# Where the first chunk's ELU takes its second step: VectorE's clamp against ScalarE's Relu, in an attention and feed-forward kernel

## The chip, the cores and the metric

One core of one Trainium2 chip. The metric is the device time of one execution in microseconds, as the median of several runs. TensorE is PE in the profile, VectorE is DVE, ScalarE is ACT, GpSimd is POOL; PEld is PE's loading of weights, SP issues DMAs.

## The reference, cut to what matters

```
# attention over q, k, v (4 x 8 heads x 768 x 64), window 16, plus 24 block summaries
a = exp(scores_all - max); a = a / (sum(a) + 1e-09); x = a @ v_all        # -> x (3072, 512)
# feed-forward
h = x @ w_in                                                               # (3072, 2048)
g = where(h > 0, h, exp(minimum(h, 0)) - 1)                                # ELU
out = g @ w_out                                                            # (3072, 512)
```

## The kernel before, in words

The 3072 rows of x are worked in six chunks of 512. For each chunk the 2048 hidden columns are taken in 16 tiles f of 128. One tile is 12 matmuls of 512 columns into the PSUM tile `h` (layer 1), the ELU from `h` to the SBUF tile `e`, the split of `e` into a rounded part `gh` and a rest `gl`, and 12 matmuls of layer 2 that add to four output banks. Every product is made of three, from high and low parts of both operands.

The first chunk is different from the other five. In its time the 32 weight tiles (j = 0 to 31; tile f uses j = 2f-1 in layer 1 and j = 2f+2 in layer 2) are still being loaded and converted: POOL makes the low bits (word `X.j`, line 136), ACT scales the exponent into a PSUM bank (`M.j`, line 141), DVE joins both (`S.j`, lines 145 and 148), ACT (three times POOL) rounds the high part (`H.j`, line 154), POOL subtracts for the low part (`L.j`, line 157). In between, the attention of the coming chunks runs in groups g of two units with halves h: `gsc` scores on PE (531), `glow` mask and minimum on DVE (168), `ge` exponentials and their sums on ACT (176), `gz` adds 1e-9 and takes the reciprocal of the sums on DVE (181, 182), `gn` scales the rows on POOL (185), `gtr` transposes on PE (194), `gpc` copies them from PSUM (550), `gval` the values on PE (567), `gxh` and `gxl` the split of the result on ACT and DVE (574, 581). Scores and transposes use the same two PSUM banks (`a0`, `a1`) as the exponent step `M.j`, so each must be read out before the other writes.

In this chunk the order of every engine's queue is the order of the words of the string `FIRST` (lines 40 to 72), written out by hand; line 730 runs them. The words of a tile f are, with the functions that they call:
- `L1h.f`, `L1l.f` (`layer1_part`, 614): 8 and 4 matmuls with the weight's high and low part.
- `E.f` (`take_exp`, `exp_of`, 619): ACT, e = exp(h).
- `ts.f` (`below`, 623): DVE, e = min(e, 1) - 1.
- `stt.f` (`above`, 626): DVE, e = max(h, 0) + e.
- `G.f` (`split_high`, 631): ACT, gh = e rounded. `gl.f` (`split_rest`, 636): POOL, gl = e - gh.
- `L2a.f`, `L2b.f`, `L2c.f` (`layer2_part`, 646): 4 matmuls each, with gh and the weight's high part, with gl and the high part, with gh and the low part. The words stand in the order a, c, b in the first tiles and mostly a, b, c later.

Tiles `e`, `gh`, `gl` and `cv` have two buffers each. From tile 16 on (chunks 1 to 5, the loop from line 748) the same functions `exp_of`, `below`, `above`, `split_high` and `split_rest` are called; there only PE and SP keep the program's order, and a planner orders the other engines. `exps` (line 172) and `exp` of the first units (line 349) allocate the tile `z` for the sums of exponentials.

Of the kernel before, what the change touches and what calls it, by code (L numbers as in the profile page):

```python
# [17 lines left out]
F32 = mybir.dt.float32  # L18
# [14 lines left out]
UW = 4  # L33
# [12 lines left out]
    tr.2.0 q.1 mv.0.1.1 z.3 ptc.2.0.1 X.0 w.5 tr.2.1 mv.1.2.1 X.1 tr.1.0 ptc.2.1.1 val.0 norm.3.0 ptc.1.0.0 M.0  # L46
    M.1 S.0 norm.3.1 val.1 mv.0.3.1 xh.0 w.6 X.2 S.1 tr.3.0 xh.1 X.3 tr.3.1 ptc.3.0.1 sk.1 X.4 val.2 ptc.3.1.1
    xl.0 H.0.1 w.7 xl.1 val.3 xh.2 H.1.1 xl.2 L.0 w.8 first.0 xh.3 M.2 xl.3 L.1 first.1 M.3 sk.2 S.2 first.2 X.5
    w.9 first.3 S.3 H.2.1 M.4 L1h.1 E.0 L.2 w.10 ts.0 H.3 stt.0 L.3 L1l.1 sk.3 S.4 G.0 E.1 gl.0 L2a.0 w.11 M.5
    L2c.0 M.6 S.5 X.6 H.4 w.12 L2b.0 X.7 ts.1 H.5 L.4 L1h.2 sv.0 M.7 stt.1 L.5 w.13 G.1 S.6 L1l.2 gl.1 S.7 L2a.1  # L50
    H.6 w.14 L2c.1 L.6 H.7 sv.1 L2b.1 E.2 ks.3 L.7 K.2 vm.0 vm.1 gsc.0 ts.2 X.8 stt.2 L1h.3 X.9 glow.0.0 G.2
    X.10 glow.0.1 M.8 gl.2 ge.0.0 L1l.3 S.8 q.2 L2a.2 w.15 X.11 E.3 gz.0.0 X.12 L2c.2 H.8 ts.3 w.16 M.9 L.8
    L2b.2 stt.3 M.10 S.9 L1h.4 G.3 sv.2 gn.0.0 ge.0.1 S.10 gl.3 L1l.4 gz.0.1 L2a.3 E.4 gn.0.1 M.11 ts.4 L2c.3
    H.9 stt.4 H.10 L2b.3 L.9 vs.1 G.4 gtr.0.0 L.10 L1h.5 S.11 gl.4 ks.2 H.11 L1l.5 gpc.0.0.1 ks.0 L.11 M.12
    gtr.0.1 ks.1 L2a.4 gpc.0.1.1 X.13 M.13 S.12 L2b.4 X.14 E.5 L2c.4 pm.2 S.13 H.12 pm.3 gval.0 X.15 X.16 ts.5
    H.13 gsc.1 w.17 w.18 sv.3 L.12 stt.5 w.19 G.5 L1h.6 glow.1.0 L.13 gxh.0 glow.1.1 M.14 w.20 gl.5 gxl.0 L1l.6
    M.15 ge.1.0 S.14 w.21 L2a.5 L2b.5 S.15 E.6 w.22 H.14 L2c.5 X.17 ts.6 H.15 L.14 L1h.7 w.23 M.16 gz.1.0 stt.6
    M.17 L.15 S.16 w.24 G.6 L1l.7 ge.1.1 gl.6 L2a.6 S.17 K.3 E.7 X.18 L2b.6 H.16 gz.1.1 gn.1.0 ts.7 L2c.6 L.16
    stt.7 gtr.1.0 vs.2 L1h.8 G.7 q.3 gn.1.1 H.17 vs.0 w.25 gpc.1.0.1 gl.7 vs.3 M.18 L1l.8 S.18 w.26 gtr.1.1 E.8
    X.19 L2a.7 gpc.1.1.1 L.17 ts.8 M.19 w.27 L2b.7 stt.8 X.20 L2c.7 S.19 G.8 X.21 w.28 gval.1 gl.8 w.29 gsc.2  # L60
    gxh.1 X.22 H.18 gxl.1 H.19 L1h.9 L.18 glow.2.0 w.30 M.20 L.19 w.31 ge.2.0 L1l.9 S.20 X.23 L2a.8 glow.2.1 E.9
    X.24 L2b.8 H.20 ts.9 ge.2.1 L.20 L2c.8 stt.9 gz.2.0 mmul G.9 L1h.10 gz.2.1 mact mm gl.9 M.21 M.22 S.21
    L1l.10 gn.2.0 L2a.9 gn.2.1 S.22 M.23 E.10 L2b.9 X.25 H.21 ts.10 X.26 L2c.9 H.22 stt.10 L.21 gtr.2.0 G.10
    L1h.11 gpc.2.0.1 L.22 S.23 M.24 L1l.11 gl.10 S.24 H.23 gtr.2.1 L.23 L2a.10 gpc.2.1.0 H.24 L2b.10 M.25 L.24
    E.11 S.25 L2c.10 X.27 gval.2 K.4 q.4 ts.11 X.28 H.25 stt.11 L.25 gsc.3 G.11 gxh.2 L1h.12 gl.11 glow.3.1
    glow.3.0 ge.3.1 gxl.2 X.29 L1l.12 X.30 M.26 L2a.11 gz.3.1 E.12 gn.3.1 S.26 L2b.11 ge.3.0 L2c.11 ts.12 H.26
    stt.12 L1h.13 M.27 L.26 G.12 S.27 M.28 gl.12 L1l.13 gz.3.0 M.29 L2a.12 S.28 gn.3.0 E.13 H.27 L2b.12 X.31
    ts.13 H.28 L2c.12 L.27 stt.13 gtr.3.0 L.28 L1h.14 S.29 gpc.3.0.1 M.30 G.13 S.30 L1l.14 H.29 gl.13 gtr.3.1
    L2a.13 L.29 gpc.3.1.1 M.31 L2b.13 H.30 S.31 L2c.13 E.14 L.30 gval.3 ts.14 stt.14 gsc.4 gxh.3 H.31 gxl.3 G.14
    L1h.15 L.31 glow.4.0 ge.4.0 gl.14 L1l.15 L2a.14 E.15 ts.15 L2b.14 stt.15 L2c.14 glow.4.1 G.15 gl.15 ge.4.1  # L70
    gz.4.1 gz.4.0 gn.4.1 gn.4.0
"""
# [3 lines left out]
def attn_elu_ffn(ctx: ExitStack, tc: tile.TileContext, qT, kT, vT, v, w_in, w_out, out):  # L76
    nc = tc.nc
    B, NP, _, S = qT.shape
# [13 lines left out]
    scale = 1.0 / math.sqrt(D)  # L92
# [3 lines left out]
    att = ctx.enter_context(tc.tile_pool(name="att", bufs=2))  # L96
# [74 lines left out]

    def exps(sm, mx, z=None):
        if z is None:
            z = att.tile([P, UW, 1], F32, tag="z", name="z", bufs=4)
        for t in range(UW):
            nc.scalar.activation(out=sm[:, t, :], in_=sm[:, t, :], func=AF.Exp, bias=mx[:, t, :], scale=-1.0,  # L176
                                 accum_out=z[:, t, :])
        return z
# [27 lines left out]
    def put_maxima(b, p):  # L206
        nc.gpsimd.tensor_copy(out=kw[p][:, :, KB:KC], in_=ks_all[b][:, p:p + 1, :].broadcast_to([P, UW, NS]))
# [9 lines left out]
    def first_units():  # L217
# [5 lines left out]
        ks = ks_all[0]  # L223
# [15 lines left out]
        mxs, zs, banks_of, o_of = {}, {}, {}, {}  # L239
# [349 lines left out]
    hs = {}  # L589
# [101 lines left out]
    with tc.manual_schedule(engines=set(engines.values())):  # L691
        do = first_units()
        convs, sources, es = {}, {}, {}
        copies = (nc.vector.tensor_copy, nc.scalar.copy)

        def conversion(j):
            if j not in convs:
                convs[j] = Conversion(j)
            return convs[j]

        def load_sum(p, src):
            sources[src is vT, p] = load_summary(1, p, src, spares[src is vT][p])

        def take_exp(n):
            es[n] = exp_of(hs[n])

        do |= {
            "w": lambda j: load(order[j]), "q": load_queries, "sk": lambda p: load_sum(p, kT),
            "sv": lambda p: load_sum(p, vT),
            "K": group_windows,  # L710
            "pm": lambda g: [put_maxima(1, units[2 * g][1] + i) for i in range(2)],
            "ks": lambda p: summary(1, p, kT, sources.pop((False, p))),
            "vs": lambda p: summary(1, p, vT, sources.pop((True, p))),
            "mmul": lambda: mean_products(1, "a1"), "mact": lambda: mean_copy(1),
            "mm": lambda: [put_means(1, p, vw[p]) for p in range(NP)],
            "X": lambda j: conversion(j).low_bits(), "M": lambda j: conversion(j).exponent(),
            "S": lambda j: conversion(j).join(), "H": lambda j, pool=0: conversion(j).high(nc.gpsimd.tensor_copy if pool else nc.scalar.copy),
            "L": lambda j: conversion(j).rest(),
            "L1h": lambda n: layer1_part(n, 0), "L1l": lambda n: layer1_part(n, 1),
            "L2a": lambda n: layer2_part(n, 0), "L2b": lambda n: layer2_part(n, 1), "L2c": lambda n: layer2_part(n, 2),  # L720
            "E": take_exp, "ts": lambda n: below(es[n]), "stt": lambda n: above(es[n], hs[n]),
            "G": lambda n: split_high(0, n, es[n]), "gl": lambda n: split_rest(0, n, es[n]),
            "gsc": group_scores, "glow": group_low, "ge": group_exps,
            "gz": lambda g, h: reciprocals(z_of[g, h]), "gn": lambda g, h: scale_rows(sm_of[g, h], z_of.pop((g, h))),
            "gtr": group_transposes, "gpc": lambda g, h, i: group_copy(g, h, copies[i]),
            "gval": group_values, "gxh": group_high, "gxl": group_rest,
        }
# [17 lines left out]
    with tc.manual_schedule(engines={engines["PE"], engines["SP"]}):  # L745
        pending = None
        last = NCH * NF - 1
        for n in range(NF, NCH * NF):
            c, f = divmod(n, NF)
            g, step = divmod(n, 4)  # L750
            h_ps = layer1(c, f)
            e = exp_of(h_ps)
# [14 lines left out]
            if n in summaries:  # L767
                b, p, src = summaries[n]
# [62 lines left out]
```

## Time and profile before

| | us |
|---|---|
| median of 3 runs | 626.95 (626.69 to 627.38) |
| the profiled execution | 626.43 |
| its span in the profile | 624.7 |
| PE busy | 616.7 (99% of the span) |
| DVE busy | 268.4 (43%) |
| ACT busy | 272.7 (44%) |
| POOL busy | 249.5 (40%) |

PE's busy time is modelled and covers waits shorter than its pipeline; where PE really stood is read from the starts of its matmuls. The shares of the other engines are means over a first fifth in which they are nearly full and a remainder in which they are about a third full.

### The profile page before, as it was taken

The numbers are of one execution on the slowest core, as the hardware profiler recorded it, in microseconds if no ns is written. First come the engines' busy times: TensorE is split into PE (matmuls) and PEld (weight loads), VectorE is DVE, ScalarE is ACT, GpSimd is POOL, SyncE is SP. The second block draws the span as 40 slices with busy tenths as digits, with TensorE's granted clock in tenths as the row PEclk, the third lists the DMA queues.
The fourth block names the chain that finished last, engine by engine and source line by source line (L and its number), as shares of the span: only waits on it lengthen the run. The fifth ranks groups of instructions, "written<-read, shape, count | busy, mean of one in ns | idle before, by whom it ended". The sixth has DMA issues, their size and how long they took to land.

```text
span 624.7 us, 11284 instructions
## 1 busy us (share of the span) xinstructions
PE 616.7 (99%) x4251; PEld 503.3 (81%) x4251; DVE 268.4 (43%) x853; ACT 272.7 (44%) x745; POOL 249.5 (40%) x266
## 2 busy tenths in 40 slices
PE   9999999999999999999999999999999999999997
PEld 6678778888888888888888888888888888888885
DVE  7789988743153432331543433314323232211222
ACT  5858676754243343442434434425334333222222
POOL 4999899742232332323323323233233231222221
PEclk9999999999999999999999999999999999999999
DMA  8998962142004405220053132402211000100001
GB/s 319 337 383 255 292 236 74 38 133 54 11 27 142 117 28 173 68 64 1 27 155 119 42 101 60 117 0 73 82 45 40 2 1 0 68 0 1 1 0 67
DMA packets 63549, 58.62 MB, mean 94 GB/s; under 512 B 22648, under 2 KB 54904, under 8 KB 63496
## 3 DMA queue, kind: packets, MB, share of 16 engines
q1 hardware_dynamic: 60184, 52.02, 27.3%
q10 hardware_dynamic: 3312, 5.90, 2.6%
q8 instruction: 33, 0.54, 0.4%
q14 instruction: 20, 0.16, 0.1%
HBM read 50.82 MB, written 6.29 MB: 91 GB/s over the span
## 4 chain that ended last, share of the span: by engine, by line
PE 86%; DVE 3%; issue 1%; ACT 0%; DVEq 0%; ACTq 0%
PE h L603 36%; PE o L656 35%; PE h L614 3%; PE o_ps L567 3%; PE o L646 3%; PE s L531 3%; PE t_ps L194 3%; DVE sh L145 1%; DVE e L623 1%; DVE cv L148 0%; DVE vst L495 0%; DVE e L626 0%; DVE z L181 0%; DVE sm L168 0%; DVE xl L581 0%
## 5 line engine op out<-in xcount | busy, mean ns | idle before, releaser
L636 POOL TENSOR_TENSOR gl<-e,gh 128x512 fp32r<-128x512 f32 x96 | 123.7, 1289 | 278.5 <-ACT gh L631 209.2
L603 PE MATMUL h<-xh,w 128*128 128x512 f32 x640 | 214.1, 395 | 0.0
L656 PE MATMUL o<-w,gh 128*128 128x512 f32 x648 | 164.7, 392 | 0.0
L623 DVE TENSOR_SCALAR e<-e 128x512 f32<-128x512 f32 x96 | 46.6, 485 | 253.6 <-ACT e L619 252.0
L603 PEld LDWEIGHTS h<-xh,w 128*128 128x128 f32 x640 | 120.1, 188 | 27.0 <-issue 2.4
L656 PEld LDWEIGHTS o<-w,gh 128*128 128x128 f32 x648 | 120.5, 188 | 24.3
L619 ACT ACTIVATE e<-h 128x512 f32<-128x512 f32 x96 | 56.9, 592 | 166.7 <-PE h L603 159.7
L603 PE MATMUL h<-xl,w 128*128 128x512 f32 x320 | 124.5, 389 | 0.0
L631 ACT CAST gh<-e 128x512 fp32r<-128x512 f32 x96 | 59.6, 621 | 97.2 <-DVE e L626 97.1
L656 PE MATMUL o<-w,gl 128*128 128x512 f32 x324 | 89.6, 389 | 0.0
L656 PEld LDWEIGHTS o<-w,gl 128*128 128x128 f32 x324 | 60.8, 188 | 12.7
L185 POOL TENSOR_TENSOR sm<-sm,z 128x480 f32<-128x480 f32 x40 | 42.8, 1073 | 67.9 <-DVE z L182 33.3
L603 PEld LDWEIGHTS h<-xl,w 128*128 128x128 f32 x320 | 60.2, 188 | 11.4
L626 DVE SCALAR_TENSOR_TENSOR e<-h,e 128x512 f32<-128x512 f32 x96 | 66.4, 691 | 3.3
L176 ACT ACTIVATE sm<-sm,mx 128x120 f32<-128x120 f32 x160 | 61.0, 383 | 15.3 <-DVE mx L168 15.3
L157 POOL TENSOR_TENSOR w<-cv,w 128x512 fp32r<-128x512 f32 x32 | 41.8, 1322 | 5.4 <-ACT w L154 4.6
L614 PE MATMUL h<-xh,w 128*128 128x512 f32 x120 | 40.5, 399 | 0.0
L581 DVE TENSOR_TENSOR xl<-o_ps,xh 128x256 fp32r<-128x256 f32 x40 | 15.1, 419 | 46.8 <-ACT xh L574 46.8
L168 DVE CUSTOM_DVE_ANT_0 sm<-s,mask 128x120 f32<-128x120 f32 x160 | 34.0, 277 | 2.0 <-PE s L531 1.9
L646 PE MATMUL o<-w,gh 128*128 128x512 f32 x120 | 32.1, 395 | 1.0 <-ACT gh L631 0.9
L176 ACT ACTIVATION_READ_ACCUMULATOR sm<-sm,mx 128x1 f32 x160 | 30.0, 187 | 0.0
L550 ACT COPY pt<-t_ps 120x512 f32<-120x512 f32 x39 | 22.8, 584 | 12.8 <-PE t_ps L194 12.8
(105 smaller groups left out, 554.4 us busy)
## 6 DMA issues: line engine op xcount, KB each, us to landing
raw_w<-in_w_in_dram SPq DMA_DIRECT2D x16, 512.0 KB, 9.5
raw_w<-in_w_out_dram SPq DMA_DIRECT2D x16, 512.0 KB, 8.7
qbd<-in_qT_dram SPq DMA_DIRECT2D x20, 256.0 KB, 2.8
out_dram<-ot ACTq DMA_DIRECT2D x20, 256.0 KB, 2.2
kw<-in_kT_dram SPq DMA_DIRECT2D x24, 144.0 KB, 3.2
vw<-in_v_dram SPq DMA_DIRECT2D x24, 144.0 KB, 2.9
n<-in_kT_dram SPq DMA_DIRECT2D x16, 192.0 KB, 2.3
n<-in_vT_dram SPq DMA_DIRECT2D x16, 192.0 KB, 2.4
```

What stands on the lines that cost most here:

```text
L157: nc.gpsimd.tensor_tensor(out=self.w[:, 1, :], in0=self.cv, in1=self.w[:, 0, :].bitcast(F32), op=ALU.subtract)
L176: nc.scalar.activation(out=sm[:, t, :], in_=sm[:, t, :], func=AF.Exp, bias=mx[:, t, :], scale=-1.0, accum_out=z[:, t, :])
L185: nc.gpsimd.tensor_tensor(out=sm, in0=sm, in1=z.broadcast_to([P, UW, KC]), op=ALU.mult)
L603: nc.tensor.matmul(h_ps, w[:, a, cols], bb[:, cc, :], start=(k == 0), stop=(k == 3 * NCC - 1))
L614: nc.tensor.matmul(h_ps, w[:, lo, cc * P:(cc + 1) * P], bb[:, cc, :], start=(lo, cc, i) == (0, 0, 0), stop=(lo, cc) == (1, NCC - 1))
L619: nc.scalar.activation(out=e, in_=h_ps, func=AF.Exp)
L623: nc.vector.tensor_scalar(out=e, in0=e, scalar1=1.0, scalar2=-1.0, op0=ALU.min, op1=ALU.add)
L626: top = nc.vector.scalar_tensor_tensor(out=e, in0=h_ps, scalar=0.0, in1=e, op0=ALU.max, op1=ALU.add)
L631: nc.scalar.copy(out=gh, in_=e)
L636: nc.gpsimd.tensor_tensor(out=gl, in0=e, in1=gs[(c, f)][0].bitcast(F32), op=ALU.subtract)
L646: nc.tensor.matmul(o_acc[0][s], gs[(0, f)][a][:, s * P:(s + 1) * P], w[:, bb, :], start=(f, part) == (0, 0), stop=False)
L656: nc.tensor.matmul(o_acc[c][s], a[:, s * P:(s + 1) * P], w[:, bb, :], start=first and f == 0, stop=last and f == NF - 1)
```

## The change

In the first chunk `ts.f` calls a new function `gap`, on ACT: e = relu(1 - exp h). `stt.f` calls a new function `larger`, on DVE: e = max(-e, h). For h below 0 that is the larger of exp(h) - 1 and h, for h above 0 it is h. The word `ts.f` is moved to stand right behind `E.f` in all 16 tiles; no other word is moved. Chunks 1 to 5 keep `below` and `above`. In the whole kernel the tile `z` is allocated twice as wide, and every second word of it is used.

```diff
 (FIRST, one tile of 16; the others alike)
-    H.6 w.14 L2c.1 L.6 H.7 sv.1 L2b.1 E.2 ks.3 L.7 K.2 vm.0 vm.1 gsc.0 ts.2 X.8 stt.2 L1h.3 X.9 glow.0.0 G.2
+    H.6 w.14 L2c.1 L.6 H.7 sv.1 L2b.1 E.2 ts.2 ks.3 L.7 K.2 vm.0 vm.1 gsc.0 X.8 stt.2 L1h.3 X.9 glow.0.0 G.2
...
-    M.15 ge.1.0 S.14 w.21 L2a.5 L2b.5 S.15 E.6 w.22 H.14 L2c.5 X.17 ts.6 H.15 L.14 L1h.7 w.23 M.16 gz.1.0 stt.6
+    M.15 ge.1.0 S.14 w.21 L2a.5 L2b.5 S.15 E.6 ts.6 w.22 H.14 L2c.5 X.17 H.15 L.14 L1h.7 w.23 M.16 gz.1.0 stt.6
...
     def exps(sm, mx, z=None):
         if z is None:
-            z = att.tile([P, UW, 1], F32, tag="z", name="z", bufs=4)
+            z = att.tile([P, UW, 2], F32, tag="z", name="z", bufs=4)[:, :, 0:1]
...
-                zs[p] = att.tile([P, 2, UW, 1], F32, tag="z2", name="z2", bufs=4)
+                zs[p] = att.tile([P, 2, UW, 2], F32, tag="z2", name="z2", bufs=4)[:, :, :, 0:1]
...
+    def gap(e):
+
+        nc.scalar.activation(out=e, in_=e, func=AF.Relu, bias=1.0, scale=-1.0)
+
+    def larger(e, h_ps):
+
+        nc.vector.scalar_tensor_tensor(out=e, in0=e, scalar=-1.0, in1=h_ps, op0=ALU.mult, op1=ALU.max)
...
-            "E": take_exp, "ts": lambda n: below(es[n]), "stt": lambda n: above(es[n], hs[n]),
+            "E": take_exp, "ts": lambda n: gap(es[n]), "stt": lambda n: larger(es[n], hs[n]),
```

## Rows read from the trace of the kernel before

**Rows 1.** The page's 40 equal slices of the span (15.6 us each): busy tenths of each engine and, as PEclk, the granted TensorE clock.

```profile
PE   9999999999999999999999999999999999999997
DVE  7789988743153432331543433314323232211222
ACT  5858676754243343442434434425334333222222
PEclk9999999999999999999999999999999999999999
```

**Rows 2.** The chain of waits that ended last, its part before 135 us: start, duration, engine and line.

```profile
70.33 1.45 DVE e L623
71.78 1.18 DVE z L181
...
82.57 1.06 DVE e L623
...
85.89 1.04 PE s L531 x30
```

**Rows 3.** The timeline of PE in the first chunk: start and duration in us, line, operation, count, and in brackets the idle time before it and who ended it.

```profile
70.71 0.39 PE L614 MATMUL h<-xh,w 128*128 128x512 f32 x1
...
72.52 1.07 PE L614 MATMUL h<-xh,w 128*128 128x512 f32 x4
74.45 1.21 PE L646 MATMUL o<-w,gh 128*128 128x512 f32 x4 [0.86 <-ACT gh L631]
75.81 1.20 PE L646 MATMUL o<-w,gl 128*128 128x512 f32 x4 [0.15 <-POOL gl L636]
...
77.77 0.60 PE L194 MATMUL t_ps<-ident,sm 128*120 128x128 f32 x4
...
85.31 0.42 PE L531 MATMUL s<-kw,qbd 64*64 64x120 f32 x2
85.89 1.04 PE L531 MATMUL s<-kw,qbd 64*64 64x120 f32 x30 [0.16 <-DVE cv L148]
86.86 0.50 PE L614 MATMUL h<-xh,w 128*128 128x512 f32 x1
...
92.51 0.47 PE L614 MATMUL h<-xh,w 128*128 128x512 f32 x1
...
98.43 0.48 PE L614 MATMUL h<-xh,w 128*128 128x512 f32 x1
...
105.64 1.05 PE L531 MATMUL s<-kw,qbd 64*64 64x120 f32 x32
106.62 0.50 PE L614 MATMUL h<-xh,w 128*128 128x512 f32 x1
```

**Rows 4.** The timeline of DVE, same columns.

```profile
65.16 0.28 DVE L168 CUSTOM_DVE_ANT_0 sm<-s,mask 128x120 f32<-128x120 f32 x1 [0.92 <-PE s L531]
...
69.64 0.69 DVE L148 SCALAR_TENSOR_TENSOR cv<-raw_w,sh 128x512 uint32<-128x512 uint32 x1
70.25 1.53 DVE L623 TENSOR_SCALAR e<-e 128x512 f32<-128x512 f32 x1
71.70 1.25 DVE L181 TENSOR_SCALAR z<-z 128x4 f32<-128x4 f32 x1
...
73.08 0.66 DVE L626 SCALAR_TENSOR_TENSOR e<-h,e 128x512 f32<-128x512 f32 x1
...
82.48 1.13 DVE L623 TENSOR_SCALAR e<-e 128x512 f32<-128x512 f32 x1
...
85.05 0.69 DVE L148 SCALAR_TENSOR_TENSOR cv<-raw_w,sh 128x512 uint32<-128x512 uint32 x1
```

**Rows 5.** The timeline of POOL, same columns.

```profile
70.20 2.72 POOL L157 TENSOR_TENSOR w<-cv,w 128x512 fp32r<-128x512 f32 x2 [0.75 <-ACT w L154]
74.47 1.29 POOL L636 TENSOR_TENSOR gl<-e,gh 128x512 fp32r<-128x512 f32 x1 [1.55 <-ACT gh L631]
75.84 0.67 POOL L136 TENSOR_SCALAR raw_w<-raw_w 128x512 uint32<-128x512 uint8 x1
76.59 0.99 POOL L185 TENSOR_TENSOR sm<-sm,z 128x480 f32<-128x480 f32 x1
...
82.03 1.30 POOL L157 TENSOR_TENSOR w<-cv,w 128x512 fp32r<-128x512 f32 x1
```

**Rows 6.** The groups by line over the whole span: line, engine, operation, count, then busy us and mean ns of one, then the idle time before them.

```profile
L623 DVE TENSOR_SCALAR e<-e 128x512 f32<-128x512 f32 x96 | 46.6, 485 | 253.6 <-ACT e L619 252.0
...
L271 ACT ACT_TABLE_LOAD x1 | 1.3, 1283 | 1.7 <-PEq L820 1.7
```

**Rows 7.** The timeline of ACT, same columns as for PE.

```profile
69.03 0.57 ACT L619 ACTIVATE e<-h 128x512 f32<-128x512 f32 x1
69.51 0.61 ACT L154 CAST w<-cv 128x512 fp32r<-128x512 f32 x1
70.42 0.62 ACT L154 CAST w<-cv 128x512 fp32r<-128x512 f32 x1 [0.30 <-DVE cv L148]
70.95 1.19 ACT L141 ACTIVATE sh<-raw_w 128x512 f32<-128x512 f32 x2
73.78 0.62 ACT L631 CAST gh<-e 128x512 fp32r<-128x512 f32 x1 [1.64 <-DVE e L626]
...
96.60 1.13 ACT L154 CAST w<-cv 128x512 fp32r<-128x512 f32 x2
```

More of the change, by code (lines that the diff above doesn't have):

```diff
@@ L48 @@
     xl.0 H.0.1 w.7 xl.1 val.3 xh.2 H.1.1 xl.2 L.0 w.8 first.0 xh.3 M.2 xl.3 L.1 first.1 M.3 sk.2 S.2 first.2 X.5
-    w.9 first.3 S.3 H.2.1 M.4 L1h.1 E.0 L.2 w.10 ts.0 H.3 stt.0 L.3 L1l.1 sk.3 S.4 G.0 E.1 gl.0 L2a.0 w.11 M.5
-    L2c.0 M.6 S.5 X.6 H.4 w.12 L2b.0 X.7 ts.1 H.5 L.4 L1h.2 sv.0 M.7 stt.1 L.5 w.13 G.1 S.6 L1l.2 gl.1 S.7 L2a.1
-    H.6 w.14 L2c.1 L.6 H.7 sv.1 L2b.1 E.2 ks.3 L.7 K.2 vm.0 vm.1 gsc.0 ts.2 X.8 stt.2 L1h.3 X.9 glow.0.0 G.2
-    X.10 glow.0.1 M.8 gl.2 ge.0.0 L1l.3 S.8 q.2 L2a.2 w.15 X.11 E.3 gz.0.0 X.12 L2c.2 H.8 ts.3 w.16 M.9 L.8
@@ L53 @@
-    L2b.2 stt.3 M.10 S.9 L1h.4 G.3 sv.2 gn.0.0 ge.0.1 S.10 gl.3 L1l.4 gz.0.1 L2a.3 E.4 gn.0.1 M.11 ts.4 L2c.3
+    w.9 first.3 S.3 H.2.1 M.4 L1h.1 E.0 ts.0 L.2 w.10 H.3 stt.0 L.3 L1l.1 sk.3 S.4 G.0 E.1 ts.1 gl.0 L2a.0 w.11
+    M.5 L2c.0 M.6 S.5 X.6 H.4 w.12 L2b.0 X.7 H.5 L.4 L1h.2 sv.0 M.7 stt.1 L.5 w.13 G.1 S.6 L1l.2 gl.1 S.7 L2a.1
+    H.6 w.14 L2c.1 L.6 H.7 sv.1 L2b.1 E.2 ts.2 ks.3 L.7 K.2 vm.0 vm.1 gsc.0 X.8 stt.2 L1h.3 X.9 glow.0.0 G.2
+    X.10 glow.0.1 M.8 gl.2 ge.0.0 L1l.3 S.8 q.2 L2a.2 w.15 X.11 E.3 ts.3 gz.0.0 X.12 L2c.2 H.8 w.16 M.9 L.8
@@ L54 @@
+    L2b.2 stt.3 M.10 S.9 L1h.4 G.3 sv.2 gn.0.0 ge.0.1 S.10 gl.3 L1l.4 gz.0.1 L2a.3 E.4 ts.4 gn.0.1 M.11 L2c.3
     H.9 stt.4 H.10 L2b.3 L.9 vs.1 G.4 gtr.0.0 L.10 L1h.5 S.11 gl.4 ks.2 H.11 L1l.5 gpc.0.0.1 ks.0 L.11 M.12
-    gtr.0.1 ks.1 L2a.4 gpc.0.1.1 X.13 M.13 S.12 L2b.4 X.14 E.5 L2c.4 pm.2 S.13 H.12 pm.3 gval.0 X.15 X.16 ts.5
+    gtr.0.1 ks.1 L2a.4 gpc.0.1.1 X.13 M.13 S.12 L2b.4 X.14 E.5 ts.5 L2c.4 pm.2 S.13 H.12 pm.3 gval.0 X.15 X.16
     H.13 gsc.1 w.17 w.18 sv.3 L.12 stt.5 w.19 G.5 L1h.6 glow.1.0 L.13 gxh.0 glow.1.1 M.14 w.20 gl.5 gxl.0 L1l.6
-    M.15 ge.1.0 S.14 w.21 L2a.5 L2b.5 S.15 E.6 w.22 H.14 L2c.5 X.17 ts.6 H.15 L.14 L1h.7 w.23 M.16 gz.1.0 stt.6
@@ L58 @@
-    M.17 L.15 S.16 w.24 G.6 L1l.7 ge.1.1 gl.6 L2a.6 S.17 K.3 E.7 X.18 L2b.6 H.16 gz.1.1 gn.1.0 ts.7 L2c.6 L.16
+    M.15 ge.1.0 S.14 w.21 L2a.5 L2b.5 S.15 E.6 ts.6 w.22 H.14 L2c.5 X.17 H.15 L.14 L1h.7 w.23 M.16 gz.1.0 stt.6
+    M.17 L.15 S.16 w.24 G.6 L1l.7 ge.1.1 gl.6 L2a.6 S.17 K.3 E.7 ts.7 X.18 L2b.6 H.16 gz.1.1 gn.1.0 L2c.6 L.16
     stt.7 gtr.1.0 vs.2 L1h.8 G.7 q.3 gn.1.1 H.17 vs.0 w.25 gpc.1.0.1 gl.7 vs.3 M.18 L1l.8 S.18 w.26 gtr.1.1 E.8
-    X.19 L2a.7 gpc.1.1.1 L.17 ts.8 M.19 w.27 L2b.7 stt.8 X.20 L2c.7 S.19 G.8 X.21 w.28 gval.1 gl.8 w.29 gsc.2
+    ts.8 X.19 L2a.7 gpc.1.1.1 L.17 M.19 w.27 L2b.7 stt.8 X.20 L2c.7 S.19 G.8 X.21 w.28 gval.1 gl.8 w.29 gsc.2
@@ L61 @@
     gxh.1 X.22 H.18 gxl.1 H.19 L1h.9 L.18 glow.2.0 w.30 M.20 L.19 w.31 ge.2.0 L1l.9 S.20 X.23 L2a.8 glow.2.1 E.9
-    X.24 L2b.8 H.20 ts.9 ge.2.1 L.20 L2c.8 stt.9 gz.2.0 mmul G.9 L1h.10 gz.2.1 mact mm gl.9 M.21 M.22 S.21
-    L1l.10 gn.2.0 L2a.9 gn.2.1 S.22 M.23 E.10 L2b.9 X.25 H.21 ts.10 X.26 L2c.9 H.22 stt.10 L.21 gtr.2.0 G.10
+    ts.9 X.24 L2b.8 H.20 ge.2.1 L.20 L2c.8 stt.9 gz.2.0 mmul G.9 L1h.10 gz.2.1 mact mm gl.9 M.21 M.22 S.21
+    L1l.10 gn.2.0 L2a.9 gn.2.1 S.22 M.23 E.10 ts.10 L2b.9 X.25 H.21 X.26 L2c.9 H.22 stt.10 L.21 gtr.2.0 G.10
@@ L64 @@
     L1h.11 gpc.2.0.1 L.22 S.23 M.24 L1l.11 gl.10 S.24 H.23 gtr.2.1 L.23 L2a.10 gpc.2.1.0 H.24 L2b.10 M.25 L.24
[L65 to L68, printed above, removed]
@@ L69 @@
-    L2a.13 L.29 gpc.3.1.1 M.31 L2b.13 H.30 S.31 L2c.13 E.14 L.30 gval.3 ts.14 stt.14 gsc.4 gxh.3 H.31 gxl.3 G.14
+    E.11 ts.11 S.25 L2c.10 X.27 gval.2 K.4 q.4 X.28 H.25 stt.11 L.25 gsc.3 G.11 gxh.2 L1h.12 gl.11 glow.3.1
+    glow.3.0 ge.3.1 gxl.2 X.29 L1l.12 X.30 M.26 L2a.11 gz.3.1 E.12 ts.12 gn.3.1 S.26 L2b.11 ge.3.0 L2c.11 H.26
+    stt.12 L1h.13 M.27 L.26 G.12 S.27 M.28 gl.12 L1l.13 gz.3.0 M.29 L2a.12 S.28 gn.3.0 E.13 ts.13 H.27 L2b.12
+    X.31 H.28 L2c.12 L.27 stt.13 gtr.3.0 L.28 L1h.14 S.29 gpc.3.0.1 M.30 G.13 S.30 L1l.14 H.29 gl.13 gtr.3.1
@@ L70 @@
+    L2a.13 L.29 gpc.3.1.1 M.31 L2b.13 H.30 S.31 L2c.13 E.14 ts.14 L.30 gval.3 stt.14 gsc.4 gxh.3 H.31 gxl.3 G.14
     L1h.15 L.31 glow.4.0 ge.4.0 gl.14 L1l.15 L2a.14 E.15 ts.15 L2b.14 stt.15 L2c.14 glow.4.1 G.15 gl.15 ge.4.1
```

## The prediction, made before the changed kernel was run

> **What bounds the kernel now.** I read the 40 slices first. PE is at 9 in all but the last, at the full granted clock, while DVE and ACT are nearly full in the first six or seven slices and a third full after them [rows 1]. So nothing done to the ELU can pay unless PE really stands still somewhere, and the page's busy time cannot show that. The chain of waits can: followed back from the end it is PE's own matmuls down to 85.9 us, and only before that does it pass through DVE. Its two longest pieces there are the clamp `ts` (1.45 us) and the first operation on the sums `z` (1.18 us), one behind the other; a third, again a clamp, stands at 82.57, and the last foreign link hands over to the scores of group 2 at 85.89 [rows 2]. From there on the time can't fall.
>
> The starts of PE's matmuls give the size. Eight matmuls of L1h.7 start from 70.71 to 72.52, so one takes 0.226 us, and L2a.6 should have started at 72.52 + 4 x 0.226 = 73.43. It started at 74.45, waiting for gh: 1.02 us lost. L2b.6 should have followed at 75.36 and came at 75.81, waiting for gl: 0.45. The scores of group 2 took from 85.31 to 86.86 = 1.55, where those of group 3 took 105.64 to 106.62 = 0.98: 0.57, waiting for DVE to read out the bank of S.19. As a check on the total: two tiles with one whole group ran from 70.71 to 86.86 = 16.15 us, and the same work from 92.51 to 106.62 took 14.11. **So 2.0 us are there to be had, all before 86.9** [rows 3].
>
> Why gh of tile 6 was late: DVE was through with S.15 at 70.33 and began ts.6 at 70.25, which took 1.53, then the z operation on four elements took 1.25, and stt.6 came at 73.08 [rows 4]. Both slow ones end as POOL's two subtractions do: 70.20 to 72.92, one of about 1.3 after the other. The clamp at 82.48 lies likewise over POOL's subtraction from 82.03 to 83.33 [rows 5]. As the trace has it, these two kinds of DVE instruction stand until POOL is between instructions. Over the span the clamp averages 0.485 [rows 6], so these are exceptions, but they fall where PE has no lead.
>
> **The change part by part.**
>
> The clamp leaves DVE in 16 tiles: about 0.49 each by its mean [rows 6], 1.53 and 1.13 in the two places on the chain. Only those two count; elsewhere PE has work in hand and DVE merely idles longer.
>
> The Relu comes to ACT in 16 tiles. No row shows a Relu. The nearest are exp of the same shape, 0.57 from PSUM, and the cast, 0.62 from SBUF to SBUF [rows 7]; the upper bound is 0.69, the two-input DVE operation on the same shape [rows 4]. I take 0.62, the cast's, because Relu too reads and writes SBUF; issued back to back these occupy ACT for about 0.55. A value below 0.57 is excluded, as the same number of elements passes the same engine.
>
> The Trainium skill, page "ScalarE: Activation LUTs", section "Rules for kernel authors", says the opposite of this move: relu, max and min belong on VectorE, which is faster per element. At rest the trace agrees (0.485 against about 0.62). By the rule each tile's chain would grow by some 0.13 us, and the sum below would be nothing or a little worse; the rows at 70.25 and 82.48 are what speaks against it here.
>
> Tile 6, step by step, all before it being unchanged because DVE waits 0.92 us for group 1's scores at 65.16 and will wait longer, whatever it has saved by then [rows 4]. ACT: E.6 at 69.03 to 69.60, ts.6 to 70.25, then H.14 to 70.8 and H.15 to 71.3 (0.6 later than before), M.16 and M.17 to 72.4 [rows 7]. DVE: S.15 to 70.33, z, then stt.6 at about 70.6 to 71.3, against 73.08 before [rows 4]. G.6 therefore no longer waits for DVE but for ACT's own queue: 72.3 to 72.9. L2a.6 starts at 73.43: **-1.0**.
>
> What is late next: gl.6. POOL's L.14 and L.15 wait for the casts, so they run from 70.85 to 73.4 instead of 70.20 to 72.92; gl.6 from 73.5 to 74.8 [rows 5]. L2b.6, due at 74.35, starts at about 74.85: its wait stays at 0.5 where it was 0.45. Then X.18 (0.67) and the row scaling (0.99) end at 76.6 on POOL, in time for PE's transposes at 76.65, which stood at 77.77 [rows 3, 5]: **-1.1 so far**, and all that follows PE moves with it.
>
> Group 2's scores: with the z operation, the clamps of tiles 7 and 8 and the wait of tile 6 gone, DVE reaches S.19 behind ACT's M.19 (transposes done near 80.3, ts.8 and the copy before it, M.19 to 82.3) and is through at 83.8, against 85.74 [rows 4]; PE wants the bank at 84.2. The wait of 0.57 goes: **-1.6**.
>
> Given back: H.21, the cast before L1h.11, ended at 97.2 for a start at 98.43 [rows 3, 7], a slack of 1.2. ACT's queue follows PE's values of group 1, which come 1.1 earlier, but has ts.9 and ts.10 (1.1) ahead of H.21, so it ends about where it did, and PE comes 1.6 earlier: **+0.3** (0 if the queue's idle microsecond before that absorbs both, 0.5 if not at all).
>
> The double-spaced z: its own cost is nothing that shows; it writes and reads the same four or eight numbers. Whether it ends the waits of that operation no row shows. The bounds are 0 and 1.25 per instance [rows 4]. I take it as worth 0 in the sum: in the changed order the z operation starts at 70.35, before L.14 can (70.85), so it would find POOL between instructions in either form.
>
> Tiles 0 to 5: ts.0 no longer lies against POOL's L.2, worth 0.1 at most; costed at nothing, since PE's waits before 40 us are for POOL's own queue. The `stt` keeps its form, one PSUM and one SBUF operand, 0.66 to 0.69 [rows 4]. Chunks 1 to 5 keep their functions, and PE, which sets the end, has nothing to gain; a new order of the other engines there is covered by their being a third full [rows 1]; if that cover were gone, one late gh would cost up to 1 us, as at 74.45.
>
> **Sum.** -1.0 - 0.1 - 0.5 + 0.3, rounded from the steps, is -1.4 (between -2.1 with every wait gone and -0.9 if gl.6 and H.21 take more). The profiled execution took 626.43, its span 624.7 and 1.7 around it: 625.0. The median of the runs shown stands 0.5 above that execution: 625.5.
>
> **The rivals.**
>
> *Given back on ACT and POOL.* The wait for gh turns into a wait for gl: H.14 and H.15 are 0.6 later, POOL is full, and each 0.3 more on either side falls on PE directly. For it: PE's waits for gl exist already [rows 3]. Against it: L.14 and L.15 only have to make up 0.5 of the 1.55 that POOL stood before gl.6 [rows 5]. With -1.0 shrunk to -0.5, the transposes waiting as well and 0.5 lost at H.21, the gain is 0 to 0.9: about 626.5.
>
> *The z operation still waits.* The Trainium skill, page "VectorE: DVE Perf Modes", section "What auto-detection actually checks", makes the two-port mode depend on SBUF operands and an even or equal outermost count, and names no step; by that the doubled spacing changes nothing. As a mechanism of this kernel: if L.14 starts before the z operation, that one ends at 72.15, stt.6 at 72.9, G.6 at 73.5, and L2a.6 loses 0.1 to 0.2: 625.7. That is inside my forecast, and its waits are not the ones that decide.
>
> *ACT becomes the bound (slower).* ACT is at 5 to 8 tenths in slices 2 to 8 [rows 1]; 0.55 in each tile of about 6 us adds one tenth. It decides once the casts H reach PE later than their tiles, that is where the slack of 1.2 at H.21 is used up in tile after tile. From tile 9 to 15, seven tiles losing 0.55 each cost 3.9, less 1.6 gained: 629.2. Against it: ACT itself waits for PE and DVE in that stretch, which is idle time that the Relu fills.
>
> *The Relu brings its own table load.* The one load in the trace took 1.28 us [rows 6]. Two per tile, 16 times, are 41 us on ACT, which has some 25 to spare: near 643. The same skill page, section "Table sets: the hidden batching unit", says that relu is in every set, by which this would not happen; no run here shows it yet.
>
> **How the numbers follow.** Forecast (gain 0.9 to 2.1, with the waiting z in it) 0.68; given back 0.25; ACT the bound 0.05; table loads 0.02. About 0.2%, 1.25 us, is what a measurement of this kernel can tell from no change; of the forecast's 0.68, 0.55 lies beyond it. So faster 0.55, same 0.13 + 0.25 = 0.38, slower 0.07. The range 624.7 to 626.6 holds the forecast with every wait gone (-2.1, and 0.1 for tile 0) and more than half of the case in which the gain is given back; what it leaves out is about 0.18.
>
> **What would show it.** Right: L2a.6 follows L1l.6 at once, stt.6 starts within 0.5 us of S.15's end, G.6 stands behind M.17, the scores of group 2 take 1.0, Relu lasts near 0.62, one table load. Wrong: a wait of PE for gh or for a cast between 85 and 130 us, a wait for gl.6 beyond 0.6, or the part before 70 us moving at all.

## The result: 631.36 us, slower, and the profile after

The changed kernel takes **631.36 us** (median of 5 runs, 630.97 to 631.98) against 626.80 for the kernel before beside it (5 runs, 626.57 to 627.38): a ratio of 1.0072 [1.0061, 1.0082]. Forecast were 625.5 (624.7 to 626.6) and "faster". The profiled execution took 631.36 as well, its span 629.6, so the change costs 4.9 us of span where 1.4 were to be gained.

The first chunk first, where the change was made. PE of the kernel after, in the stretch of [rows 3] (start, duration, line, operation, count, and in brackets the idle time and who ended it):

```profile
73.54 1.10 PE L614 MATMUL h<-xh,w 128*128 128x512 f32 x4
74.48 1.08 PE L654 MATMUL o<-w,gh 128*128 128x512 f32 x4
75.40 1.12 PE L654 MATMUL o<-w,gl 128*128 128x512 f32 x4
...
77.28 0.60 PE L194 MATMUL t_ps<-ident,sm 128*120 128x128 f32 x4
...
84.88 1.07 PE L531 MATMUL s<-kw,qbd 64*64 64x120 f32 x32
85.88 0.50 PE L614 MATMUL h<-xh,w 128*128 128x512 f32 x1
...
97.13 0.60 PE L194 MATMUL t_ps<-ident,sm 128*120 128x128 f32 x4
97.96 0.50 PE L614 MATMUL h<-xh,w 128*128 128x512 f32 x1 [0.23 <-ACT w L154]
...
105.20 1.05 PE L531 MATMUL s<-kw,qbd 64*64 64x120 f32 x32
106.19 0.50 PE L614 MATMUL h<-xh,w 128*128 128x512 f32 x1
```

L2a.6 follows L1l.6 at once, L2b.6 follows it at once, and the scores of group 2 take 84.88 to 85.88 = 1.00 where they took 1.55. All three waits of [rows 3] are gone. One came: L1h.11, behind transposes that take 0.36 elsewhere, starts 0.83 after them, so 0.47 late. DVE and ACT at tile 6, beside [rows 4] and [rows 7]:

```profile
70.22 0.69 DVE L148 SCALAR_TENSOR_TENSOR cv<-raw_w,sh 128x512 uint32<-128x512 uint32 x1
70.83 0.16 DVE L181 TENSOR_SCALAR z<-z 128x4 f32<-128x4 f32 x1
...
71.12 0.66 DVE L631 SCALAR_TENSOR_TENSOR e<-e,h 128x512 f32<-128x512 f32 x1
...
91.28 1.34 DVE L181 TENSOR_SCALAR z<-z 128x4 f32<-128x4 f32 x1
```

```profile
70.22 0.63 ACT L627 ACTIVATE e<-e 128x512 f32<-128x512 f32 x1
70.76 1.12 ACT L154 CAST w<-cv 128x512 fp32r<-128x512 f32 x2
71.79 1.18 ACT L141 ACTIVATE sh<-raw_w 128x512 f32<-128x512 f32 x2
72.91 0.60 ACT L639 CAST gh<-e 128x512 fp32r<-128x512 f32 x1
```

This is the order that was forecast: stt.6 right behind S.15, and G.6 behind M.17 instead of behind DVE. So the changed chunk does what it should, and at 106.19 PE is still 0.43 us ahead of before (106.62), although group 1's scores had come 0.57 later (DVE met them at 65.73 instead of 65.16).

The loss is behind it, where no function was changed. The chain of waits (start, duration, engine, tile, line, count), before and then after, over one stretch of the second chunk:

```profile
134.62 2.72 PE o L656 x12
137.34 2.72 PE h L603 x12
140.06 2.72 PE o L656 x12
...
156.88 2.72 PE h L603 x12
```

```profile
134.49 2.72 PE o L664 x12
137.21 2.79 PE h L603 x12
140.01 2.74 PE o L664 x12
...
156.91 2.79 PE h L603 x12
```

Both chains are PE alone here, with no wait in them. Twelve matmuls of layer 1 take 2.79 instead of 2.72, those of layer 2 2.74 instead of 2.72. The groups by line give the total over chunks 1 to 5 (busy us, mean ns of one | idle time before), before and after:

```profile
L603 PE MATMUL h<-xh,w 128*128 128x512 f32 x640 | 214.1, 395 | 0.0
L656 PE MATMUL o<-w,gh 128*128 128x512 f32 x648 | 164.7, 392 | 0.0
L603 PE MATMUL h<-xl,w 128*128 128x512 f32 x320 | 124.5, 389 | 0.0
...
L656 PE MATMUL o<-w,gl 128*128 128x512 f32 x324 | 89.6, 389 | 0.0
```

```profile
L603 PE MATMUL h<-xh,w 128*128 128x512 f32 x640 | 216.8, 399 | 0.0
L664 PE MATMUL o<-w,gh 128*128 128x512 f32 x648 | 165.5, 393 | 0.0
L603 PE MATMUL h<-xl,w 128*128 128x512 f32 x320 | 126.0, 394 | 0.0
...
L664 PE MATMUL o<-w,gl 128*128 128x512 f32 x324 | 89.6, 389 | 0.0
```

2.7 + 0.8 + 1.5 + 0.0 = 5.0 us. And counted from the first whole twelve of layer 2 in the chain (L656, after L664), the rest of the span is 629.6 - 134.49 = 495.1, where it was 624.7 - 134.62 = 490.1: 5.0 as well. **The loss is the same matmuls taking longer, with no idle time**, and the granted clock is 9 tenths or more in every slice, as before:

```profile
PEclk9999999999999999999999999999999999999999
```

What can do this to untouched matmuls? For the tiles that they read, the built programs give one difference. `z2` is 4 buffers of 64 bytes per partition where it was 4 of 32, so every tile that is allocated after it lies 128 bytes higher: `e`, `gh`, `gl`, `cv` and all weights. `x` (xh, xl) is allocated ahead of it and stays:

```
bytes per partition     before            after
xh                      38464, 46656      38464, 46656
xl                      54848, 63040      54848, 63040
gh                      89664, 91712      89792, 91840
weights (w1_5)          97856             97984
```

Before, x, gh, gl and the weights all lie a whole number of 2048 bytes apart. After, x lies 128 off from the rest. Layer 1 reads x and the weights; layer 2 reads gh or gl and the weights.

### The profile page after: what moved, and what is told of

Read it like the earlier page. It is cut to its first block, busy times and chain, and to the rows that moved or that the text cites. A ratio compares the mean times of both kernels' runs of the same rounds, so it can differ in the third digit from the quotient of the medians.

```text
span 629.6 us, 11270 instructions
## 1 busy us (share of the span) xinstructions
PE 621.9 (99%) x4251; PEld 503.3 (80%) x4251; DVE 255.8 (41%) x837; ACT 282.3 (45%) x761; POOL 248.6 (39%) x266
## 4 chain that ended last, share of the span: by engine, by line
PE 84%; ACT 2%; issue 0%; DVE 0%; DVEq 0%
PE h L603 36%; PE o L664 35%; PE o_ps L567 3%; PE s L531 3%; PE t_ps L194 2%; PE h L614 2%; PE o L654 2%; ACT sm L176 0%; ACT w L154 0%; ACT sh L141 0%; ACT e L627 0%; ACT e L619 0%; DVE sh L145 0%; DVE cv L148 0%; ACT ots L690 0%
## 5 line engine op out<-in xcount | busy, mean ns | idle before, releaser
L603 PE MATMUL h<-xh,w 128*128 128x512 f32 x640 | 216.8, 399 | 0.0
L664 PE MATMUL o<-w,gh 128*128 128x512 f32 x648 | 165.5, 393 | 0.0
L664 PEld LDWEIGHTS o<-w,gh 128*128 128x128 f32 x648 | 120.6, 188 | 25.8
L623 DVE TENSOR_SCALAR e<-e 128x512 f32<-128x512 f32 x80 | 34.8, 435 | 255.7 <-ACT e L619 254.2
L603 PE MATMUL h<-xl,w 128*128 128x512 f32 x320 | 126.0, 394 | 0.0
L664 PE MATMUL o<-w,gl 128*128 128x512 f32 x324 | 89.6, 389 | 0.0
L664 PEld LDWEIGHTS o<-w,gl 128*128 128x128 f32 x324 | 60.8, 188 | 12.7
L634 DVE SCALAR_TENSOR_TENSOR e<-h,e 128x512 f32<-128x512 f32 x80 | 55.3, 692 | 2.8
L614 PE MATMUL h<-xh,w 128*128 128x512 f32 x120 | 41.0, 402 | 0.2 <-ACT w L154 0.2
```

The lines of the kernel that those rows point to most:

```text
L603: nc.tensor.matmul(h_ps, w[:, a, cols], bb[:, cc, :], start=(k == 0), stop=(k == 3 * NCC - 1))
L614: nc.tensor.matmul(h_ps, w[:, lo, cc * P:(cc + 1) * P], bb[:, cc, :], start=(lo, cc, i) == (0, 0, 0), stop=(lo, cc) == (1, NCC - 1))
L664: nc.tensor.matmul(o_acc[c][s], a[:, s * P:(s + 1) * P], w[:, bb, :], start=first and f == 0, stop=last and f == NF - 1)
```

## The experiments

The theory: **place**. The wider tile's only harm is that it moves the tiles behind it; matmuls slow down by the distance between the tiles that PE reads. The rivals: **the wide z itself** (its accumulating writes or strided reads disturb PE or DVE), and **the ELU** (the Relu and the moved words leave ACT or POOL in PE's way in all chunks). Within place: distance, or the address of one of the tiles. "Off" below is by how many bytes the weights lie away from x, measured from before, and "cadence" is what twelve matmuls of layer 1 and layer 2 take in the chain of waits, where no transposes or scores stand between them (single groups differ by 0.01).

| run | off | median us (runs) | ratio | cadence |
|---|---|---|---|---|
| after | 128 | 631.36 (5) | 1.0072 [1.0061, 1.0082] | 2.79, 2.74 |
| e1: ELU alone | 0 | 625.54 (10) | 0.9981 [0.9969, 0.9993] | 2.72, 2.72 |
| e2: wide z alone | 128 | 632.47 (4) | 1.0084 [1.0069, 1.0099] | 2.79, 2.73 |
| e3: padding alone | 128 | 632.76 (4) | 1.0088 [1.0072, 1.0103] | 2.79, 2.74 |
| e4: after, all moved 384 | 0 | 626.39 (10) | 0.9983 [0.9972, 0.9995] | 2.72, 2.72 |
| e5: weights alone | 128 | 637.58 (2) | 1.0168 [1.0149, 1.0187] | 2.79, 2.79 |
| e6: 32 | 32 | 634.33 (1) | | 2.80, 2.75 |
| e10: 64 | 64 | 634.42 (1) | | 2.80, 2.74 |
| e11: 192 | 192 | 632.59 (1) | | 2.76, 2.77 |
| e7: 256 | 256 | 626.43 (1) | | 2.72, 2.72 |
| e12: all moved 64 | 0 | 627.09 (1) | | 2.72, 2.72 |
| e13: x 128, rest 256 | 128 | 632.82 (1) | | 2.79, 2.74 |
| e14: x 64, rest 256 | 192 | 634.10 (1) | | 2.76, 2.77 |
| e9: after, moved to 256 | 256 | 625.98 (10) | 0.9979 [0.9969, 0.9989] | 2.72, 2.72 |
| e8: Relu to tile 8 | 0 | 625.17 (12) | 0.9977 [0.9966, 0.9988] | 2.72, 2.72 |

The kernel before stood at 627.31 beside e1 to e4, 626.78 beside e5 to e8, 627.01 beside e9 to e11 and 626.34 (one run) beside e12 to e14. Times of single runs also carry their start: the first values of the attention (L371), ahead of any feed-forward, begin at 23.18 us in e13, 23.42 in e11 and 24.87 in e14, which is 1.45 of the 1.51 us between e14 and e11. So the cadence decides there, not the time.

**e1 and e2: the two halves of the change, each by itself.** e1 is after with the sums as they were; e2 is before with the wide sums.

```diff
 (e1, from after)
-            z = att.tile([P, UW, 2], F32, tag="z", name="z", bufs=4)[:, :, 0:1]
+            z = att.tile([P, UW, 1], F32, tag="z", name="z", bufs=4)
-                zs[p] = att.tile([P, 2, UW, 2], F32, tag="z2", name="z2", bufs=4)[:, :, :, 0:1]
+                zs[p] = att.tile([P, 2, UW, 1], F32, tag="z2", name="z2", bufs=4)
 (e2, from before: the same lines the other way)
```

> The changed kernel with the sums of exponentials back to adjacent words: only the Relu and the larger-of remain. Theory 1 (distance): the wider z moved the weight tiles by 128 bytes against xh and xl, and that made layer 1's matmuls slow; here the distance is as in the kernel before, so twelve matmuls of layer 1 take 2.72 us again and the first chunk keeps what it saved: about 625.4 us (625.0 to 626.0), 1.0 to 1.8 below the kernel before. Rival 2 (ScalarE): the 16 Relus and the new order of ScalarE's queue caused the loss: about 631. Rival 3 (the z operations themselves, at a step of two words): 625.4 as well, so this run does not tell it from theory 1.

> The kernel before with only the wider z. Theory 1 (distance): 2.79 us for twelve matmuls of layer 1 in all 96 tiles, so 96 x 0.07 = 6.7 less what hides in the first chunk: about 632 (631 to 633.5). Rival 2 (ScalarE): 626.8, as before. Rival 3 (z operations): about 632.

e1 is faster than before, e2 slower (1.0084, after 1.0072; the intervals overlap). The ELU is cleared; the whole loss comes with the two lines on `z`. The chain of e1, in the stretch shown above:

```profile
136.29 2.72 PE h L603 x12
139.01 2.72 PE o L664 x12
...
155.83 2.72 PE h L603 x12
```

**e3: the move without the wide z.** Before, with 128 bytes of unused padding behind `vst`, the tile that is allocated just after `z2`.

```diff
-            vst_all[b] = att.tile([P, NP, BLK], F32, tag="vst", name="vst", bufs=1)
+            vst_all[b] = att.tile([P, NP * BLK + 32], F32, tag="vst", name="vst", bufs=1)[:, 0:NP * BLK].rearrange("p (n k) -> p n k", k=BLK)
```

> The kernel before, z unchanged, with the unrelated tile vst 128 bytes longer per partition, so that e, gh, gl, cv and all weight tiles lie 128 bytes further from xh and xl and nothing else changes. Theory 1 (distance): as the run with z alone, about 632, layer 1 at 2.79 per twelve, layer 2 at 2.72. Rivals 2 and 3: 626.8.

Padding that nobody reads or writes costs as much as the wide z (632.76 and 632.47), so the width itself costs nothing that shows. On DVE neither, by the groups by line of e2 and then e3 (busy us, mean ns of one):

```profile
L181 DVE TENSOR_SCALAR z<-z 128x4 f32<-128x4 f32 (+1 forms) x44 | 10.2, 232 | 22.6 <-ACT sm L176 22.5
```

```profile
L181 DVE TENSOR_SCALAR z<-z 128x4 f32<-128x4 f32 (+1 forms) x44 | 10.2, 233 | 22.6 <-ACT sm L176 22.5
```

**e4: the whole change, with the distances as before.** `z` and `z2` get a pool of their own ahead of `att`, and `vst` 256 bytes of padding: x, gh, gl and weights all lie 384 bytes higher.

```diff
+    sums = ctx.enter_context(tc.tile_pool(name="sums", bufs=4))
-            z = att.tile([P, UW, 2], F32, tag="z", name="z", bufs=4)[:, :, 0:1]
+            z = sums.tile([P, UW, 2], F32, tag="z", name="z", bufs=4)[:, :, 0:1]
...
-            vst_all[b] = att.tile([P, NP, BLK], F32, tag="vst", name="vst", bufs=1)
+            vst_all[b] = att.tile([P, NP * BLK + 64], F32, tag="vst", name="vst", bufs=1)[:, 0:NP * BLK].rearrange("p (n k) -> p n k", k=BLK)
```

> The changed kernel complete, wide z included, but z lies ahead of xh and xl and vst is 256 bytes longer, so the distance from xh to the weight tiles is that of the kernel before, while every one of these tiles lies 384 bytes higher than there. Theory 1 (distance): about 625.4, layer 1 at 2.72. A variant of it (the weights' own address counts, not the distance): 631. Rival 2 (ScalarE) and rival 3 (z operations): 631.

With the wide z kept and the distances restored the cadence is 2.72 again and the kernel is faster than before. The rival of the wide z falls.

**e5: the weights moved against everything.** Before, with each of the two `gl` buffers 64 bytes longer: the weights lie 128 off both from x and from gh and the first gl; the second gl lies 64 off from gh.

```diff
-        gl = ffn.tile([P, CH], F32R, tag="gl", name="gl")
+        gl = ffn.tile([P, CH + 16], F32R, tag="gl", name="gl")[:, 0:CH]
```

> The kernel before with the tile gl 64 bytes longer per partition, so that only the weight tiles move, by 128 bytes, and e, gh, cv and the first gl stay. It asks which pair of tiles counts. If it is the two operands of one matmul: layer 1 (stationary weights moved, xh and xl not) at 2.79 us per twelve, and now layer 2 too (stationary gh not moved, moving weights moved) above 2.72, at 2.79 if it behaves alike: 632 for layer 1 alone, about 638 to 639 with both. If it is the other engines' tiles e, gh, cv against xh: both layers 2.72, 626.8.

Now layer 2 slows down as layer 1 does, and the loss doubles, 10.8 us:

```profile
136.44 2.78 PE o L656 x12
139.22 2.78 PE h L603 x12
```

**e6, e7, e10, e11: other sizes.** The padding of e3 with 32, 256, 64 and 192 bytes.

> As the run that moved the later tiles by 128 bytes, with 32 bytes. If any distance that is no multiple of 2048 bytes costs the same: layer 1 at 2.79 us per twelve, about 632. If the cost grows with the distance: between 2.72 and 2.79, about 628. If there is a finer period of 32 bytes: 2.72, 626.8.

> The same with 256 bytes. Any distance alike: 2.79, about 632. Growing with the distance: about 2.86, 638. A period of 256 bytes: 2.72, 626.8.

> The kernel before with vst 64 bytes longer. With a period of 256 bytes and the same cost at every distance between: layer 1 at 2.79 us per twelve, about 632. If 64 bytes are a unit of the period: 2.72, 626.8.

> The kernel before with vst 192 bytes longer. With a period of 256 bytes and the same cost at every distance between: 2.79, about 632; the same as with 64 bytes, if the distance counts in both directions alike.

32 bytes are as bad as 64, and 256 is free: not any move costs, and a small one is no cheaper. If 256 is a period, the distance does not count alike in both directions: 192 bytes, 64 short of it, give 2.76 and 2.77, 64 bytes 2.80 and 2.74. And layer 2 also lost (2.73 to 2.77 in e2, e3, e6, e10 and e11; 2.72 was expected of e3), though gh, gl and the weights had moved together. Distance between a matmul's own two tiles does not explain that.

**e12, e13, e14: distance or address, and layer 2's part.** `warm`, a tile of the first pool, is 64, 128 and 64 bytes longer, which moves everything; e13 and e14 add 128 and 192 bytes behind `vst`.

```diff
-        warm = const.tile([P, 1], F32, name="warm")
+        warm = const.tile([P, 17], F32, name="warm")[:, 0:1]
```

> The kernel before with a tile at the very front of the memory 64 bytes longer: x, gh, gl and the weights all move by 64 bytes, and every distance between them stays. By the distance alone: 2.72 per twelve matmuls in both layers, 626.4. By the place of the operands itself (64 bytes off, as in the run with 64 bytes ahead of gh): 2.80 and 2.74, about 634.

> The kernel before with x moved by 128 bytes, gh, gl and the weights by 256. By the distance alone: layer 1 (x against weights, 128 apart) 2.79 and layer 2 (gh against weights, none) 2.72, 631 to 632. By the place of the weights alone (256, which was free): 2.72 in both, 626.4. If layer 2 suffers from x lying off the other tiles, it stays at 2.74 although its own operands are where they were free: 632.7.

> The kernel before with x moved by 64 bytes, gh, gl and the weights by 256: x stands 192 ahead of them, where in the run with 64 bytes ahead of gh it stood 64 behind and in that with 192 it stood 192 behind. By the distance alone, counted in 256: layer 1 as with 192 bytes (64 the other way), 2.76 to 2.80, layer 2 2.72, 630 to 632. If layer 2 suffers from x lying off, 2.74 to 2.77 there too: 632.6 to 634.4. By the place of the weights alone: 2.72 in both, 626.4.

e12 has gh, gl and the weights at the places that were bad in e10, with the distances of before: its cadence is 2.72 again. e13 has gh, gl and weights where they were free in e7, with x 128 away: it behaves as e3. The chains of e12 and then e13 at one stretch:

```profile
404.99 2.72 PE o L656 x12
407.71 2.72 PE h L603 x12
410.43 2.72 PE o L656 x12
```

```profile
410.66 2.79 PE h L603 x12
413.45 2.73 PE o L656 x12
416.19 2.79 PE h L603 x12
```

e14 has both layers at 2.76 and 2.77 as e11, which has the same distance of 192 at other addresses. So **it is the distance, not the address**. And layer 2's loss is x's too. From the starts in the traces: in the 44 layer-2 groups of chunks 1 to 5 that stand between two groups of layer 1, the mean time from one matmul's start to the next is 226.8, 226.4 and 226.9 ns for the first three before, and 231.3, 230.4 and 229.3 after; from the fourth on both lie between 226.4 and 226.9. Layer 2 loses on the matmuls right behind layer 1's, which read x. At 32 and 64 bytes it is the first five (228.3 to 235.0 ns in e6), at 192 nearly all of the first ten (226.7 to 234.6 in e11).

**e9 and e8: versions that keep the gain.** e9 is after with 128 bytes more behind `vst`, so that the tiles lie 256 higher in all. e8 is e1 with the Relu in tiles 0 to 8 alone; from tile 9 on the clamp stays with DVE, in its old place in the order.

```diff
 (e8, from e1)
-            "E": take_exp, "ts": lambda n: gap(es[n]), "stt": lambda n: larger(es[n], hs[n]),
+            "E": take_exp, "ts": lambda n: gap(es[n]) if n <= 8 else below(es[n]),
+            "stt": lambda n: larger(es[n], hs[n]) if n <= 8 else above(es[n], hs[n]),
```

> The changed kernel complete, with wide z, and the tile vst 128 bytes longer, so that the later tiles lie 256 bytes further from xh and xl than in the kernel before. If the cost depends on the distance of a matmul's two operands with a period of 256 bytes: layer 1 at 2.72 us per twelve, about 625.5, 1.0 to 1.8 below the kernel before. If the free distance of 256 bytes was chance of that one run: 631 or more.

> z narrow as in the kernel before; the Relu only in tiles 0 to 8, the clamp on VectorE in its old place from tile 9 on. It takes the two Relus away that stand ahead of the cast for L1h.11. If the wait for that cast (0.46 us of matmul starts in the changed kernel) is ScalarE's queue, it goes: 0.3 to 0.5 us below the kernel with all 16 Relus and narrow z, so about 1.9 below the kernel before. If it comes from the weights' arrival or VectorE, the time is as with 16 Relus, 1.4 to 1.8 below the kernel before. What speaks for less: the z operation of 1.3 us at 91 us then lies ahead of a clamp again.

e9 cures the change as it stands with one line. e8 takes the new wait at L1h.11 away; its PE there, beside 97.13 and 97.96 after:

```profile
96.14 0.60 PE L192 MATMUL t_ps<-ident,sm 128*120 128x128 f32 x4
96.50 0.48 PE L612 MATMUL h<-xh,w 128*128 128x512 f32 x1
```

Its span is 622.8, against 623.7 for e1: of these 0.9, 0.25 stand already at L1h.9 (84.96 against 85.21), where the two kernels still run the same words, and 0.55 more at L1h.11 (96.50 against 97.30), which is that wait. The two ratios overlap, so the medians do not tell e8 from e1 or e9. All three are faster than before, and than after.

## Why the prediction was wrong, point by point

**The step that failed** is "The double-spaced z: its own cost is nothing that shows; it writes and reads the same four or eight numbers", together with "Chunks 1 to 5 keep their functions, and PE, which sets the end, has nothing to gain". Each is true as a sentence: e2 against e3 shows the width costing nothing. But the first costed the edit by its instructions alone. A tile's size is also an address for all that is allocated after it, and PE, busy at 9 tenths in all slices but the last, had something to lose: 4.2 / 80 = 0.05 us on average in each layer-1 group and 0.8 / 81 = 0.01 in each of layer 2 are the 5.0 us above. No rival held this either; the two on the slower side (ACT the bound, a table load per Relu) were other mechanisms, and their sign, with 7 in 100, was right by accident.

**The sum for the ELU was right.** e1 is the change without the shift of the tiles. Starting level with before (group 1's scores with `ks` at 64.44, before 64.49), it has

```profile
84.21 1.07 PE L531 MATMUL s<-kw,qbd 64*64 64x120 f32 x32
85.21 0.50 PE L614 MATMUL h<-xh,w 128*128 128x512 f32 x1
...
97.30 0.50 PE L614 MATMUL h<-xh,w 128*128 128x512 f32 x1 [0.25 <-ACT w L154]
```

86.86 - 85.21 = 1.65 gained at L1h.9 (forecast 1.6), and 98.43 - 97.30 = 1.13 at L1h.11, so 0.5 given back there (forecast 0.3, at most 0.5). The span is 1.0 shorter where 1.4 were forecast. Against the runs beside it e1 gained 0.0019 x 627.31 = 1.2 us [0.4, 1.9]. After kept little of this: at its first whole twelve of layer 2 it is 0.13 ahead of before (134.49 against 134.62), e1 1.05 (133.57). Of the 0.9 between them 0.6 were there at group 1's scores; the first chunk's layer 1 has the new distance too (L1h.7 to L2a.6 takes 71.69 to 74.48 = 2.79, in e1 71.12 to 73.85 = 2.73).

- *L2a.6 without its wait, -1.0*: right, in e1 and after.
- *gl.6 next late, its wait stays at 0.5*: wrong place. L2b.6 has no wait, but in e1 POOL's two subtractions ahead of gl.5 start at 65.28 instead of 64.90, and L2b.5 waits 0.37 (due 67.86 + 0.91 = 68.77, started 69.14). The net was the same, transposes at 76.66 in e1, forecast 76.65; that is luck, as the forecast held all ahead of tile 6 to be unchanged.
- *Scores of group 2, -0.5*: right, 1.00 after.
- *Relu at 0.62 (0.57 to 0.69)*: 0.633, 16 times; and one table load, so that rival falls:

```profile
L627 ACT ACTIVATE e<-e 128x512 f32<-128x512 f32 x16 | 10.1, 633 | 0.5
...
L271 ACT ACT_TABLE_LOAD x1 | 1.3, 1283 | 1.7 <-PEq L828 1.7
```

- *The z operation still waits*: true, at 91.28 for 1.34 us, though its numbers lie two words apart, over this subtraction of POOL's:

```profile
91.23 1.30 POOL L157 TENSOR_TENSOR w<-cv,w 128x512 fp32r<-128x512 f32 x1 [0.87 <-ACT w L154]
```

At tile 6 it started at 70.83, before L.14 (71.44), and took 0.16, for the reason forecast: its place in the order. As that rival said, it decides nothing.
- *ACT the bound*: refuted; e1's chain from chunk 1 on is PE at 2.72.
- Of the signs named for "wrong", two came: a wait of PE for a cast (0.47 at 97.96) and a part before 70 us that moved (0.57 in after, L2b.5 in e1). Neither is the loss: e1 has the wait for the cast and that of L2b.5, and is faster.

The Trainium skill, page "ScalarE: Activation LUTs", section "Rules for kernel authors", would have kept the relu on VectorE. At rest the trace agrees (a clamp 0.435 in the chunks that keep it, a Relu 0.633); e1 shows that the move still pays where the clamp took 1.53 over POOL's subtractions [rows 4, 5].

## What to carry to other kernels

Cost a changed tile size as a move of everything allocated behind it, not only by the instructions that touch it; where PE has no idle time, compare the cadence of matmuls that nobody edited, first of all. If such matmuls got slower at full clock and without a wait, print the addresses of their operands before and after, and try a padding that brings the distance back. Keep a run for each half of a two-part change: here one half gained 1 us and the other lost 5, and the sum showed neither.

## What the runs showed of the hardware

**The cadence of matmuls depended on how far apart in the partition the tiles lie that PE reads.** At distances of 0 and 256 bytes (beyond whole multiples of 2048) twelve matmuls of 128x512 took 2.72 us; at 32 and 64 layer 1 took 2.80, at 128 2.79 and at 192 2.76. At 0, 128 and 192 bytes other addresses gave the same (e12 and e4; e13; e14); 32, 64 and 256 were run at one address of the weights each. At the worst that is (2.80 - 2.72) / 12 = 7 ns in 227 for one. The weight load did not get longer; the loads of layer 1 before and then after:

```profile
L603 PEld LDWEIGHTS h<-xh,w 128*128 128x128 f32 x640 | 120.1, 188 | 27.0 <-issue 2.4
```

```profile
L603 PEld LDWEIGHTS h<-xh,w 128*128 128x128 f32 x640 | 120.3, 188 | 29.0 <-issue 2.4
```

188 ns each, with more idle time between them. The Trainium skill, page "TensorE: Matmul & The Clock Gate", section "Step-by-step: what each phase is for", gives TensorE two independent read ports, one for the streaming operand and one for the weight load; by that the place of one tile against the other would not matter. The runs differ from it: moving the weights alone by 128 bytes cost 10.8 us (e5).

What stays open: which two reads of PE meet. The runs show only that the tiles' distance decides and that the effect reaches three (at 128 bytes) to ten (at 192) matmuls past the last that reads x. A period of 256 bytes fits, but only 256 itself was tried beyond 192. That after and e9 began group 1's scores some 0.6 us later than before, and e1 did not, is not explained either; part of it is there before the ELU, as the attention's first values (L371) begin at 23.31 before, 23.41 in e1, 23.64 after and 24.28 in e9, and at 23.97 in e12, which changes no function.
